# Weight sums of the FFN made with the conversion and kept in DRAM, more conversion in attention, and a new order of FFN group changes

## The chip, the cores and the metric

The kernel runs on one core of a Trainium2 chip. The metric is the device time of one execution in microseconds, lower is better. The kernel before takes 1252.25 us, the median of three runs (1250.42 to 1252.28).

## The reference

Attention with a feature map, a mixture of eight experts of which each chosen token uses one, and an FFN whose hidden layer is the maximum of three products:

```python
# q, k, v: (8, 8, 576, 64); w_phi: (64, 128); x: 4608 tokens of 512; d_ff 1024 (experts), 768 (FFN)
def phi(x):
    proj = np.einsum('bhsd,df->bhsf', x, w_phi)
    proj = proj - np.max(np.abs(proj), axis=-1, keepdims=True)
    return np.concatenate([np.exp(proj), np.exp(-proj)], axis=-1)
q_p, k_p = (phi(q), phi(k))
kv = np.einsum('bhsf,bhsd->bhfd', k_p, v)
num = np.einsum('bhsf,bhfd->bhsd', q_p, kv)
den = np.einsum('bhsf,bhf->bhs', q_p, k_p.sum(2))[..., None] + 1e-06
x = num / den                                   # to 4608 x 512
do_compute = x @ w_skip > 0                     # the other tokens pass unchanged
e_idx, gate_w = argmax and softmax weight of x @ w_gate
x[mask of expert e] += gate_w * (np.maximum(x @ w1[e], 0) @ w2[e])
h = np.maximum(np.maximum(x @ ffn_w1, x @ ffn_w2), x @ ffn_w3)
out = h @ ffn_w_out
```

The FFN's weights come in as float64.

## The kernel before

**Attention** runs in 72 steps and five more to drain. A step makes two tiles of 128 tokens for a pair of heads: projections `pr` on TensorE (L553), their largest absolute value `m` (L558) and the difference `d` (L560) on VectorE, exponentials on ScalarE, then the sums `kv` and the numerators `n` on TensorE, and the division in `put_x` on VectorE. `n` has one PSUM buffer. SP loads the inputs `raw`, three chunks ahead; a chunk serves one and a half steps. After every 18 steps a pair of batches is complete, and `route` (L229 is its first reduction) finds each token's expert; its list positions are scattered by POOL (`scatter_ids`).

**The conversion.** `conv_steps` is a generator that turns the 24 float64 tiles of FFN weights, 128x512 each, into float32 and stores them in `wfd` in DRAM. A tile takes six steps: SP loads `pf`; ScalarE squares the high words into `sq` and VectorE begins `da`; two more VectorE instructions (L190, L195); then VectorE's last (L199), ScalarE's copy of the low words into `sq` (L200) and POOL's multiply and add (L201, L202); an empty step; and the store to `wfd` on SP (L205). `sq` has one buffer, `da` and `pf` two. Sixty steps of attention (6 to 65) call it once each; the rest is called from `pump` in the expert stage. Behind the 24 tiles the same generator makes the overflow lists (`make_overflow`, with one iota on POOL).

**Experts.** The experts are worked off in the order of their sizes, in blocks of up to 384 tokens. For a block POOL gathers the tokens' rows from `xa` in DRAM (`gather`), TensorE transposes them (`xt`), `layer1` makes `ht`, `layer2` the outputs, which VectorE adds to the rows (`add_y`, L964) and POOL scatters back (`put_rows`, L969). Each matmul is made of three (L486 to L488), with operands split into a rounded high and a low part: ScalarE writes the high part, VectorE subtracts it for the low one (`w_split`, L168 and L170). After every second product or so the kernel calls `pump`, which splits one more weight and then makes one step of the conversion. Once all expert weights are split, `pump` makes steps of `w1_prep`, which prepares the FFN's first weights.

**FFN.** It multiplies 2x2 blocks with seven products in place of eight, so that it needs sums of blocks of both operands. `quad1` is one set of seven products for a group of 512 tokens and one pair of weight tiles: nine pairs in each of nine groups, 81 sets; `quad2` does the same for layer 2, 18 sets. For a pair of weight tiles `Operands` loads both tiles from `wfd` into one staging buffer `stg` (of four, shared with the expert weights and `f_load`), has POOL make four sums (`sums_left`, `sums_right`, L804 to L813) into `sc`, and splits one half tile (`single`), one whole (`wide`) and two wholes of sums (`pair`) with `split` (L800 on ScalarE, L801 on VectorE). The products of a set run in the order 6, 4 (of the set before), 1 (of the next one), 5, 7, 2 (of the next one), 3. Products 1, 6, 5 and 3 accumulate in one PSUM buffer and ScalarE copies it to `pu` (L1129) after 1, 6 and 5.

Everything else of the FFN hangs on a list: `do(n, at, f)` has `f` issued behind product `at` of set `n`. `x_next` puts the next group there: `f_load` of its rows, `f_ps` and `f_xt` (two PSUM tiles of `ps_t`, which has two, and eight transposes, L1065) for half `i` = 0 and then for half 1, `x_put` for the splits of the group's operands and `x_sums` for their sums (L1080). The first group is written out by hand ahead of the loop: all transposes, all sums and splits, and then products 1 and 2 of set 0. `w1_prep` goes on with one step behind each product of sets 0 to 4, and with all the rest in set 5. `to_layer2` lists the loads and splits of layer 2's weights and of the first hidden groups in the last group of layer 1.

The order on each engine is the order in which the code issues instructions.

Of the kernel before, what the change touches and what calls it, by code (L numbers as in the profile page):

```python
# [19 lines left out]
P = 128  # L20
# [25 lines left out]
def kernel(  # L46
# [42 lines left out]
    wfd = dram.tile([NFT, P, 512], F32, name="wfd")  # L89

# [89 lines left out]
    def from_double(t, pool, i):  # L180
# [23 lines left out]
        yield  # L204
        nc.sync.dma_start(out=wfd[i], in_=af)  # L205

    conv_done = [0]

    def conv_steps(pool):
# [5 lines left out]
        nxt = start(0)  # L215
# [294 lines left out]
    with ac:  # L510
# [201 lines left out]
        for s2 in range(NS // 2 + LN):  # L712
# [61 lines left out]
    sc_p = ctx.enter_context(tc.tile_pool(name="sc", bufs=2))  # L774
# [28 lines left out]
    def sums_left(sc, x11, x12, x21, x22, eng):  # L803
        eng.tensor_tensor(out=sc[:, 2], in0=x21, in1=x22, op=ALU.add)  # L804
        eng.tensor_tensor(out=sc[:, 0], in0=sc[:, 2], in1=x11, op=ALU.subtract)
        eng.tensor_tensor(out=sc[:, 1], in0=x11, in1=x21, op=ALU.subtract)
        eng.tensor_tensor(out=sc[:, 3], in0=x12, in1=sc[:, 0], op=ALU.subtract)

    def sums_right(sc, x11, x12, x21, x22, eng):
        eng.tensor_tensor(out=sc[:, 2], in0=x12, in1=x11, op=ALU.subtract)  # L810
        eng.tensor_tensor(out=sc[:, 0], in0=x22, in1=sc[:, 2], op=ALU.subtract)
        eng.tensor_tensor(out=sc[:, 1], in0=x22, in1=x12, op=ALU.subtract)
        eng.tensor_tensor(out=sc[:, 3], in0=x21, in1=sc[:, 0], op=ALU.subtract)  # L813

# [12 lines left out]
    class Operands:  # L827


        def __init__(self, raw, side, whole, half, sums, eng=nc.vector):  # L830
            self.raw, self.side, self.whole, self.half, self.pool, self.eng = raw, side, whole, half, sums, eng
            self.blocks = {}

        def steps(self):
            return [self.sums, self.single, self.wide, lambda: self.pair(0), lambda: self.pair(2)]

        def sums(self):
            r = self.raw
            x = [[r[:, a, b * 256 : (b + 1) * 256] for b in range(2)] for a in range(2)]
            self.sc = self.pool.tile([P, 4, 256], F32, name="sc")  # L840
            if self.side == "rows":
                sums_left(self.sc, x[0][0], x[0][1], x[1][0], x[1][1], nc.gpsimd)
            elif self.side == "cols":
                sums_left(self.sc, x[0][0], x[1][0], x[0][1], x[1][1], nc.gpsimd)
            else:
                sums_right(self.sc, x[0][0], x[0][1], x[1][0], x[1][1], nc.gpsimd)

        def single(self):
            h = self.half()
            rows = self.side == "rows"  # L850
            split(h, self.raw[:, 1, 256:] if rows else self.raw[:, 0, 0:256], self.eng)
            self.blocks[4 if rows else 1] = h

        def wide(self):
            w = self.whole()
            split(w, self.raw[:, 0 if self.side == "rows" else 1], self.eng)
            a, b = {"rows": (1, 2), "cols": (2, 4), "right": (2, 3)}[self.side]
            self.blocks[a], self.blocks[b] = w[:, :, 0:256], w[:, :, 256:]

        def pair(self, c):  # L860
            w = self.whole()
            split(w, self.sc[:, c : c + 2].rearrange("p a b -> p (a b)"))
# [384 lines left out]
    def op_step(ops, key, i):  # L1247
        ops[key][i]()
# [217 lines left out]
```

## Time and profile before

| | |
|---|---|
| median of 3 runs | 1252.25 us |
| profiled execution | 1254.91 us, its span 1253.2 us |
| TensorE matmul busy | 1134.4 us, 91% of the span |
| VectorE busy | 853.6 us, 68% |
| ScalarE busy | 562.0 us, 45% |
| POOL (GpSimd) busy | 321.7 us, 26% |
| mean granted TensorE clock | 0.972 of full speed |
| chain that ended last | TensorE 42%, VectorE 6%, DMA 6%, POOL 5%, issue 4%, ScalarE 2% |

PE is TensorE, DVE VectorE, ACT ScalarE, SP the engine that issues most transfers. Attention lasts to about 370 us, the experts to about 655 us, layer 1 of the FFN to about 1090 us. A row's number in brackets is the time for which its engine stood idle ahead of it, with what ended the idle time.

### The profile page before, as it was taken

To read this page: it belongs to the slowest core of one execution; us is meant where nothing else is said; L and a number is where in the kernel's file an instruction comes from. 1 tells how busy PE (TensorE), PEld (TensorE's weight loads), DVE (VectorE), ACT (ScalarE), POOL (GpSimd) and SP (SyncE) were. 2 spreads that over 40 slices of the span, in tenths; PEclk is the share of its full clock that TensorE was granted. 3 is DMA by queue.
4 is the path that set the end of the run, shared out by engine and by line. 5 is a ranking of instruction groups with operands and counts; after the bars stand their busy time and mean duration, and the time that the engine had idled before them with its cause. 6 is when DMAs were issued, how large, how long until landed. Compare 5 with 4: busy or idle time off the path is not lost.

```text
span 1253.2 us, 34023 instructions
## 1 busy us (share of the span) xinstructions
PE 1134.4 (91%) x14212; PEld 1055.3 (84%) x14212; DVE 853.6 (68%) x1820; ACT 562.0 (45%) x1290; POOL 321.7 (26%) x356
## 2 busy tenths in 40 slices
PE   6999899898687889878997899999999999999996
PEld 5888788777576778767886899999999999999996
DVE  5889679778553575776877756556556566887772
ACT  3565555544361344455445333333333233455552
POOL 0001221212164345343154100000000000569770
PEclk9999999999799899989998999999999999999998
DMA  7555845454741665665753120220111111345541
GB/s 260 179 167 184 190 158 189 162 171 129 112 133 31 200 231 159 236 210 176 238 161 92 68 68 35 68 69 35 68 62 41 55 49 50 135 153 188 186 149 70
DMA packets 96782, 166.53 MB, mean 133 GB/s; under 512 B 20674, under 2 KB 39618, under 8 KB 96624
## 3 DMA queue, kind: packets, MB, share of 16 engines
q1 hardware_dynamic: 91904, 154.19, 38.7%
q0 software_dynamic: 4352, 8.85, 2.2%
q8 instruction: 113, 1.85, 0.6%
q10 hardware_dynamic: 368, 1.27, 0.3%
q14 instruction: 45, 0.37, 0.1%
HBM read 120.77 MB, written 45.51 MB: 133 GB/s over the span
## 4 chain that ended last, share of the span: by engine, by line
PE 42%; DVE 6%; DMA 6%; POOL 5%; issue 4%; ACT 2%; POOLq 0%; SPq 0%; ACTq 0%; DVEq 0%
PE mm L488 14%; PE mm L486 14%; PE mm L487 14%; DMA xa<-xg,ixr 4%; DMA stg<-in_w_exp_dram 1%; POOL sq L201 1%; POOL xg L468 1%; DVE sc L1080 1%; PE tp L1065 1%; POOL da L202 1%; DVE wB L801 1%; DVE w L801 1%; DVE xB L801 1%; ACT xB L800 0%; DVE mt L1114 0%
## 5 line engine op out<-in xcount | busy, mean ns | idle before, releaser
L1129 ACT ACTIVATE pu<-mm 128x256 f32<-128x256 f32 x297 | 114.4, 385 | 271.3 <-PE mm L488 248.1
L1116 DVE TENSOR_TENSOR pu<-mm,pu 128x256 f32<-128x256 f32 x162 | 68.2, 421 | 95.0 <-PE mm L488 92.2
L804 POOL TENSOR_TENSOR sc<-stg 128x256 f32<-128x256 f32 x15 | 12.3, 823 | 409.7 <-DMA stg<-hd 375.0
L579 ACT ACTIVATE e<-d 128x512 f32<-128x512 f32 x144 | 82.9, 623 | 62.9 <-DVE d L560 57.4
L633 PE MATMUL n<-kvw,q 128*64 128x74 f32 x2304 | 95.2, 235 | 15.2 <-issue 14.7
L593 PE MATMUL kv<-raw,e 128*64 128x74 f32 (+1 forms) x2560 | 97.6, 234 | 4.1 <-issue 4.0
L593 PEld LDWEIGHTS kv<-raw,e 128*64 128x64 f32 (+1 forms) x2560 | 83.9, 138 | 19.6 <-issue 17.9
L558 DVE TENSOR_REDUCE m<-pr 128x8 f32<-128x1024 f32 x72 | 87.8, 1220 | 18.0 <-PE pr L553 12.6
L633 PEld LDWEIGHTS n<-kvw,q 128*64 128x64 f32 x2304 | 85.0, 141 | 17.7 <-issue 16.4
L553 PE MATMUL pr<-wph,raw 64*64 64x128 f32 x2304 | 87.9, 289 | 9.5 <-DMA wph<-in_w_phi_dram 6.3
L486 PE MATMUL mm<-xT,w 128*128 128x256 f32 x288 | 81.8, 284 | 11.5 <-ACT pu L1129 5.9
L560 DVE TENSOR_TENSOR d<-pr,m 128x1024 f32<-128x1024 f32 x72 | 88.2, 1225 | 4.6
L201 POOL TENSOR_TENSOR sq<-sq,pf 128x512 f32<-128x512 f32 x24 | 31.7, 1319 | 227.8 <-DVE pf L199 205.8
L1114 DVE TENSOR_TENSOR mt<-mm,pu 128x256 f32<-128x256 f32 x135 | 56.4, 417 | 39.3 <-PE mm L488 38.8
L553 PEld LDWEIGHTS pr<-wph,raw 64*64 64x64 f32 x2304 | 68.3, 141 | 16.7 <-DMA raw<-in_qkv_dram 6.3
L572 ACT ACTIVATE q<-tr 128x512 f32<-128x512 f32 x72 | 42.7, 594 | 87.9 <-PE tr L570 81.7
L487 PE MATMUL mm<-xT,w 128*128 128x256 f32 x288 | 81.5, 283 | 0.0
L488 PE MATMUL mm<-xT,w 128*128 128x256 f32 x288 | 81.4, 283 | 0.0
L1117 DVE TENSOR_TENSOR mt<-mt,pu 128x256 f32<-128x256 f32 x162 | 71.8, 443 | 5.6
L487 PE MATMUL mm<-wB,w 128*128 128x256 f32 x266 | 74.5, 280 | 0.0
L488 PE MATMUL mm<-wB,w 128*128 128x256 f32 x266 | 74.5, 280 | 0.0
L486 PE MATMUL mm<-wB,w 128*128 128x256 f32 x266 | 74.4, 280 | 0.0
(278 smaller groups left out, 3800.7 us busy)
## 6 DMA issues: line engine op xcount, KB each, us to landing
raw<-in_qkv_dram SPq DMA_DIRECT2D x46, 798.0 KB
stg<-in_w_exp_dram SPq DMA_DIRECT2D x64, 512.0 KB
hd<-mt SPq DMA_DIRECT2D x27, 512.0 KB
pf<-in_w_ffn_dram SPq DMA_DIRECT2D x24, 512.0 KB
hb<-hd SPq DMA_DIRECT2D x21, 512.0 KB
xa<-xs SPq DMA_DIRECT2D x16, 576.0 KB
stg<-xa SPq DMA_DIRECT2D x18, 512.0 KB
out_dram<-mt SPq DMA_DIRECT2D x18, 512.0 KB
```

The source lines that it names most:

```text
L486: nc.tensor.matmul(out=ps, lhsT=ah, rhs=bh, start=first, stop=False, skip_group_check=on)
L487: nc.tensor.matmul(out=ps, lhsT=ah, rhs=bl, start=False, stop=False, skip_group_check=on)
L488: nc.tensor.matmul(out=ps, lhsT=al, rhs=bh, start=False, stop=last, skip_group_check=on)
L553: nc.tensor.matmul(out=pr[p0 : p0 + 64, h, 2 * s + i], lhsT=raw[k0, o + p0 : o + p0 + 64], rhs=wph[k0], start=True, stop=True,)
L558: nc.vector.tensor_reduce(out=m, in_=pr, axis=AX.X, op=ALU.max, apply_absolute_value=True)
L560: nc.vector.tensor_tensor(out=d, in0=pr, in1=m[:, :, :, None].to_broadcast([P, 2, 4, P]), op=ALU.subtract)
L579: nc.scalar.activation(out=e[:, :, :, s], in_=ds[s2][:, :, 2:4], func=AF.Exp, scale=scale)
L593: nc.tensor.matmul(out=kvps[u, b][c : c + 64, 2 * h + s], lhsT=e[p0:p1, h, i, s, c : c + 64], rhs=v[p0:p1, h], start=t == 4 * b and h + s ...
L633: nc.tensor.matmul(out=ps[p0 : p0 + 64, i, h], lhsT=q[:, s, 2 * h + i, p0 : p0 + 64], rhs=kvw[u, b][:, 2 * h + s], start=s == 0, stop=s == 1,)
L1116: nc.vector.tensor_tensor(out=tmp, in0=ps, in1=tmp, op=ALU.add)
L1117: nc.vector.tensor_tensor(out=out, in0=out, in1=tmp, op=ALU.max)
L1129: nc.scalar.activation(out=t, in_=ps, func=AF.Copy)
```

## The change

- `from_double` loses its empty step: the store to `wfd` follows one step after POOL's instructions. After every second tile POOL makes the pair's four sums into `sm` and SP stores them in a new DRAM tensor `wsm`; that takes two steps, so that a pair still takes twelve.
- Attention makes two conversion steps in each of its 60 steps.
- The FFN's weight operands no longer have POOL make sums. `Operands.load` brings for each pair, in two staging buffers, half of the sums and one tile, and then the other half and half a tile. Hidden operands of layer 2 keep their sums on POOL (`HiddenOperands`).
- `w1_prep` loads one part ahead and is listed behind each product of sets 0 to 7.
- The first group: products 1 and 2 of set 0 come before the second half of the transposes, product 6 of set 0 and product 1 of set 1 among the sums and splits.
- `x_next`: half 1 of a group starts ten products after half 0 where it started seven after.
- `to_layer2`: loads and splits of layer 2's weights in six parts, at other products. The pool `sc` moves from the expert stage to the FFN, and the first group uses it. Pairs of `w_out` tiles lie side by side in the input's layout.

```diff
-    def from_double(t, pool, i):
+    def from_double(t, pool, i, pair):
...
         nc.gpsimd.tensor_tensor(out=sq, in0=sq, in1=hi.bitcast(F32), op=ALU.mult)
         nc.gpsimd.tensor_tensor(out=af, in0=af, in1=sq, op=ALU.add)
         yield
-        yield
         nc.sync.dma_start(out=wfd[i], in_=af)
+        pair.append(af)
...
+    def sums_left(sc, x11, x12, x21, x22, eng):
+        eng.tensor_tensor(out=sc[:, 2], in0=x21, in1=x22, op=ALU.add)
+        eng.tensor_tensor(out=sc[:, 0], in0=sc[:, 2], in1=x11, op=ALU.subtract)
+        eng.tensor_tensor(out=sc[:, 1], in0=x11, in1=x21, op=ALU.subtract)
+        eng.tensor_tensor(out=sc[:, 3], in0=x12, in1=sc[:, 0], op=ALU.subtract)
...
             t, nxt = nxt, start(i + 1) if i + 1 < NFT else None
             yield
-            yield from from_double(t, pool, i)
-            conv_done[0] = i + 1
+            yield from from_double(t, pool, i, pair)
+            if i % 2:
+                yield
+                x = [v[:, c : c + 256] for v in pair for c in (0, 256)]
+                sm = pool.tile([P, 4, 256], F32, name="sm", bufs=1)
+                (sums_left if i < 18 else sums_right)(sm, *x, nc.gpsimd)
+                pair.clear()
+                yield
+                nc.sync.dma_start(out=wsm[i // 2], in_=sm.rearrange("p (a b) c -> p a (b c)", a=2))
+                conv_done[0] = i // 2 + 1
...
             if 6 <= s2 < NS // 2 - 6:
                 next(conv)
+                next(conv)
...
     class Operands:
+        def __init__(self, side, whole, half):
+            self.side, self.whole, self.half, self.blocks = side, whole, half, {}
+
+        def load(self, n, p):
+            right = self.side == "right"
+            t = stg_p.tile([P, 2, 512], F32, name="stg")
+            nc.sync.dma_start(out=t[:, 1 - n] if n == 0 else t[:, 0], in_=wsm[p, :, n])
+            if n == 0:
+                nc.sync.dma_start(out=t[:, 0], in_=wfd[2 * p + right])
+            elif right:
+                nc.sync.dma_start(out=t[:, 1, 0:256], in_=wfd[2 * p, :, 0:256])
+            else:
+                nc.sync.dma_start(out=t[:, 1, 0:256], in_=wfd[2 * p + 1, :, 256:])
+            if n == 0:
+                self.src = [t[:, 0], t[:, 1]]
+            else:
+                self.src += [t[:, 0], t[:, 1, 0:256]]
+
+        def step(self, i):
+            right = self.side == "right"
+            if i == 3:
+                h = self.half()
+                split(h, self.src[3])
+                self.blocks[1 if right else 4] = h
+            else:
+                w = self.whole()
+                split(w, self.src[i])
+                a, b = (((2, 3) if right else (1, 2)), (6, 7), ((5, 4) if right else (5, 3)))[i]
+                self.blocks[a], self.blocks[b] = w[:, :, 0:256], w[:, :, 256:]
...
     def w1_steps():
         half = halves(w1_tile)
+        ops = [Operands("left", w1_tile, half) for _ in range(9)]
+
+        def load(n):
+            p, part = divmod(n, 2)
+            if p < 9:
+                while conv_done[0] <= p:
+                    next(conv)
+                ops[p].load(part, p)
+
+        load(0)
+        yield
         for p in range(9):
-            nxt = load(p + 1) if p < 8 else None
-            yield
...
+            for part in range(2):
+                load(2 * p + part + 1)
+                if part == 0:
+                    while w1_used[0] + 4 > (freed[0] - WF + NWA + NWB if not wc_p else NWA + NWB + NWC + 4):
+                        yield
+                for i in (2 * part, 2 * part + 1):
+                    ops[p].step(i)
+                    yield
+            w1[p] = ops[p].blocks
...
         for i in range(2):
-            q = n0 + 5 + i
-            do(q, 0, f_ps, g, i)
-            do(q, 0, f_xt, g, i)
-            for at, p in ((2, 1), (3, 2), (4, 3)):
-                do(q, at, x_put, g, p, i)
-            do(q, 5, x_sums, g, i, (0,))
-            do(q, 6, x_sums, g, i, (1,))
+            q = 7 * (n0 + 5) + 10 * i
+            at = [divmod(q + t, 7) for t in range(8)]
+            do(*at[0], f_ps, g, i)
+            do(*at[0], f_xt, g, i)
+            for t, p in ((2, 1), (3, 2), (4, 3)):
+                do(*at[t], x_put, g, p, i)
+            do(*at[5], x_sums, g, i, (0,))
+            do(*at[6], x_sums, g, i, (1,))
...
-        for k, (ld, at) in enumerate(((2, 6), (4, 1), (4, 1))):
-            do(n0 + ld, at, w2_load, k)
+        for k, part, q, at in ((0, 0, 2, 6), (0, 1, 3, 1), (1, 0, 4, 0), (1, 1, 5, 0), (2, 0, 5, 5), (2, 1, 5, 5)):
+            do(n0 + q, at, w2_load, k, part)
...
             for p in (1, 2):
                 for i in range(2):
                     x_put(g0, p, i)
+            step(0, 1)
+            step(0, 2)
     for i in range(2):
         x_sums(g0, i, (0,))
     for i in range(2):
         x_put(g0, 6, i)
+    step(0, 6)
     for i in range(2):
         x_sums(g0, i, (1,))
+    step(1, 1)
     for p in (5, 7, 3, 4):
         for i in range(2):
             x_put(g0, p, i)
-    for n in range(5):
+    for n in range(8):
         for at in range(7):
             do(n, at, next, w1_prep, None)
-    do(5, 0, list, w1_prep)
```

## Rows read from the trace of the kernel before

**Rows 1.** Busy time by stretch: matmul, weight load, DVE, ACT, POOL, clock, DMA.

```profile
30.00:345.00 315.00, 284.38 (x7201) 249.36 (x7203) 248.56 (x552) 167.83 (x353) 53.03 (x50) 0.96 0.57 165
...
701.00:1075.00 374.00, 364.44 (x3059) 361.38 (x3058) 223.86 (x572) 128.66 (x362) 4.75 (x6) 1.00 0.17 59
1075.00:1240.00 165.00, 163.75 (x1381) 163.34 (x1380) 126.88 (x212) 90.29 (x210) 106.25 (x115) 1.00 0.43 147
```

**Rows 2.** Timeline of VectorE in attention: start, duration, what (first and last steps).

```profile
61.73 1.23 DVE L558 TENSOR_REDUCE m<-pr 128x8 f32<-128x1024 f32 x1
...
99.34 1.22 DVE L558 TENSOR_REDUCE m<-pr 128x8 f32<-128x1024 f32 x1
...
130.37 1.22 DVE L558 TENSOR_REDUCE m<-pr 128x8 f32<-128x1024 f32 x1
...
133.61 1.22 DVE L558 TENSOR_REDUCE m<-pr 128x8 f32<-128x1024 f32 x1
```

**Rows 3.** TensorE's waits, 470 to 656 us: total, times, longest.

```profile
PE mm L487 <- DVE xt L482: 3.4, 2, 2.0
PE mm L486 <- DVE ht L478: 2.9, 1, 2.9
PE mm L486 <- ACT ht L476: 2.4, 1, 2.4
PE mm L488 <- DVE ht L478: 2.1, 4, 0.8
```

**Rows 4.** TensorE's waits, 701 to 1240 us.

```profile
PE tp L1065 <- DVE sc L1080: 9.6, 16, 1.0
```

**Rows 5.** Timelines of TensorE, ScalarE and POOL where the FFN begins.

```profile
668.69 0.58 PE L486 MATMUL mm<-xT,w 128*128 128x256 f32 x1 [5.92 <-ACT pu L1129]
...
664.42 0.72 ACT L800 ACTIVATE xT<-mt 128x256 fp32r<-128x256 f32 x2 [2.89 <-DMA xa<-xg,ixr]
...
668.25 0.38 ACT L1129 ACTIVATE pu<-mm 128x256 f32<-128x256 f32 x1
...
659.29 1.00 POOL L969 DMA_INDIRECT xa<-xg,ixr  x1
```

**Rows 6.** TensorE's waits, 655 to 701 us.

```profile
PE mm L486 <- DVE pu L1116: 3.0, 1, 3.0
...
PE mm L486 <- DVE mt L1114: 2.0, 1, 2.0
```

**Rows 7.** Groups in attention, 30 to 330 us: busy, mean ns of one, idle before.

```profile
L190 DVE SCALAR_TENSOR_TENSOR da<-pf,da 128x512 int32<-128x512 int32 x10 | 6.8, 681 | 0.0
...
L199 DVE TENSOR_SCALAR pf<-da 128x512 int32<-128x512 int32 x10 | 4.2, 420 | 0.0
...
L229 DVE TENSOR_REDUCE lr<-lg 128x81 f32<-128x648 f32 x3 | 4.1, 1355 | 0.0
...
L184 ACT ACTIVATE sq<-pf 128x512 f32<-128x512 f32 x10 | 6.8, 684 | 0.0
```

**Rows 8.** Splits beside POOL's sums (671 to 701 us), alone (620 to 638); first sum.

```profile
L801 DVE TENSOR_TENSOR wB<-stg,wB 128x256 fp32r<-128x256 f32 x4 | 3.7, 922 | 0.0
...
L801 DVE TENSOR_TENSOR wB<-stg,wB 128x512 fp32r<-128x512 f32 x3 | 3.1, 1032 | 1.1 <-ACT wB L800 1.1
...
L170 DVE TENSOR_TENSOR wB<-stg,wB 128x512 fp32r<-128x512 f32 x11 | 7.0, 686 | 0.1
...
639.00 0.74 POOL L804 TENSOR_TENSOR sc<-stg 128x256 f32<-128x256 f32 x1 [4.65 <-DMA stg<-wfd]
```

**Rows 9.** Timelines of POOL, ScalarE and TensorE at an expert block's end.

```profile
511.81 1.05 POOL L468 DMA_INDIRECT xg<-xa,ixr  x1 [4.16 <-DMA xa<-xg,ixr]
...
515.99 0.66 ACT L184 ACTIVATE sq<-pf 128x512 f32<-128x512 f32 x1 [7.51 <-POOL da L202]
...
516.97 0.50 PE L486 MATMUL mm<-wB,ht 128*128 128x512 f32 x1 [2.40 <-ACT ht L476]
```

**Rows 10.** TensorE's waits, 411 to 470 us.

```profile
PE mm L486 <- ACT ht L476: 4.5, 3, 4.1
```

More of the change, by code (lines that the diff above doesn't have):

```diff
@@ L89 @@
     wfd = dram.tile([NFT, P, 512], F32, name="wfd")
+    wsm = dram.tile([NFT // 2, P, 2, 512], F32, name="wsm")
     def setup(load):
@@ L213, in start @@
             return t
-        nxt = start(0)
+        nxt, pair = start(0), []
         for i in range(NFT):
@@ L827 @@
     class Operands:
[L830 to L837, printed above, removed]
+        def __init__(self, side, whole, half):
+            self.side, self.whole, self.half, self.blocks = side, whole, half, {}
@@ new lines, in step, with __init__ @@
+        def step(self, i):
[9 more added lines that the diff above has]
+                self.blocks[a], self.blocks[b] = w[:, :, 0:256], w[:, :, 256:]
+    class HiddenOperands:
+        def __init__(self, raw, whole, half, pool):
+            self.raw, self.whole, self.half, self.pool, self.blocks = raw, whole, half, pool, {}
+        def step(self, i):
@@ L848, in single @@
[L848 to L858, printed above, removed]
@@ L876, in w1_steps @@
         half = halves(w1_tile)
-        def load(p):
-            while conv_done[0] < 2 * p + 2:
-                next(conv)
-            t = stg_p.tile([P, 2, 512], F32, name="stg")
-            nc.sync.dma_start(out=t, in_=wfd[2 * p : 2 * p + 2].rearrange("i p c -> p i c"))
-            return Operands(t, "rows", w1_tile, half, sc_p)
-        cur, nxt = load(0), None
+        ops = [Operands("left", w1_tile, half) for _ in range(9)]
[6 more added lines that the diff above has]
+        load(0)
         yield
-        cur.sums()
         for p in range(9):
-            nxt = load(p + 1) if p < 8 else None
-            yield
-            while w1_used[0] + 4 > (freed[0] - WF + NWA + NWB if not wc_p else NWA + NWB + NWC + 4):
-                yield
-            for f in cur.steps()[1:]:
-                f()
-                yield
-                if f == cur.wide and nxt:
-                    nxt.sums()
-            w1[p] = cur.blocks
-            cur = nxt
+            for part in range(2):
[7 more added lines that the diff above has]
+            w1[p] = ops[p].blocks
     w1_prep = w1_steps()
@@ L1196 @@
     w2_op = {}
-    def w2_load(k):
-        raw = stg_p.tile([P, 2, 512], F32, name="stg")
-        nc.sync.dma_start(out=raw, in_=wfd[18 + k : 24 : 3].rearrange("i p c -> p i c"))
-        op = Operands(raw, "right", lambda: wb_p.tile([P, 2, 512], F32R, name="wB"), w2_half, sc_p)
-        w2[k], w2_op[k] = op.blocks, op.steps()
+    for k in range(3):
+        w2_op[k] = Operands("right", lambda: wb_p.tile([P, 2, 512], F32R, name="wB"), w2_half)
+        w2[k] = w2_op[k].blocks
     h_used = [0]
@@ L1245, in x_next, with w2_load @@
             do(n0 + 9, 2 + i, x_put, g, 4, i)
+    def w2_load(k, part):
+        w2_op[k].load(part, 9 + k)
     def op_step(ops, key, i):
-        ops[key][i]()
+        ops[key].step(i)
     def to_layer2(n0):
@@ L1269, in to_layer2 @@
                 do(n0 + q, at, op_step, w2_op, k, i)
[L1270 to L1271 removed]
+        for k, (q, at) in enumerate(((6, 5), (6, 5), (7, 5))):
+            do(n0 + q, at, h_load, g1, k, stg, "stg", sb_p)
     def layer2_pools():
@@ L1290, in h_next, with step @@
                     do(*at[first + k], op_step, h_op, (g, k), s)
+    quads = [(quad1, g, p) for g in groups for p in range(9)] + [(quad2, g, m) for g in groups for m in range(2)]
+    made = {}
+    def step(n, p):
+        if 0 <= n < len(quads):
+            if n not in made:
+                f, *args = quads[n]
+                made[n] = f(*args)
+            made[n].step(p)
     g0 = groups[0]
```

72 lines of the change are left out of this document (25 added, 47 removed), and 6 rows, old and new, of tables (at, q).

## The prediction

> **What bounds the kernel now.** I read the page's first two parts, then busy time by stretch, then TensorE's waits in each stretch, and last the order of instructions at the places where TensorE stood. Three stretches differ. In attention TensorE is busy for 284.4 of 315 us, VectorE for 248.6 [rows 1]; where nothing disturbs them, nine steps take 37.61 us, 4.18 us each, and VectorE needs 3.24 us for a step that carries no conversion [rows 2]. So TensorE sets the pace there, and VectorE has a little under a microsecond to spare. In the expert stage TensorE waits for evictions: its releasers are `ht` and `xt`, which ScalarE and VectorE write [rows 3]. In the FFN it is busy for 364.4 of 374 us [rows 1], and 9.6 of the missing microseconds are one wait, 16 times [rows 4]. Layer 2 is full (163.75 of 165 us) [rows 1]. The time to be won lies in the second stretch, at the turn from experts to FFN [rows 5, 6], and in that one repeated wait.
>
> **Attention: ten more tiles converted there.** Sixty steps convert ten tiles now and twenty after. A tile has two VectorE instructions of 0.68 us and two of 0.42 us, 2.20 us, and two on ScalarE of 0.68 us, 1.37 us [rows 7]. That is 22 us more VectorE and 13.7 us more ScalarE work in 60 steps, 0.37 us of VectorE a step. A step has 3.24 us without conversion, some 0.1 us more where a new chunk is read, and would then have 0.73 us of conversion: 4.1 us on average against TensorE's 4.18 [rows 2]. It just fits, so most of it is hidden under TensorE. It fits badly in steps with both 0.68 us instructions, and beside routing, whose first reduction alone has 1.36 us, once for each of three pairs [rows 7]: what VectorE is late there TensorE's single `n` buffer passes on. I take one such reduction's length for each of the three, 4 us. Below that the bound is 0 (all hidden; nothing leaves this stretch that could make it shorter); above, everything exposed, 22 + 13.7 = 36 us; the row it is nearest to is the 3.24 us step with its 0.9 us of room, so I stay near the low end and let 12 us stand as the end of what is likely. The POOL sums (4 of 0.74 us or more for each pair) [rows 8] run while POOL is nearly idle (53 of 315 us) [rows 1]. The `wfd` store moves to one conversion step after POOL's add where it stood two behind, and holds SP's later `raw` loads while it waits; those are issued three chunks, four and a half steps or 18.8 us, ahead, which hides POOL's two instructions. If that cover went, the next late thing would be `ones_col` on ScalarE, then TensorE.
>
> The Trainium skill (SBUF — State Buffer, "Who interferes with whom") says that a VectorE instruction with two SBUF inputs and a GpSimd instruction that reads SBUF exclude each other, the later one blocked until the other ends. The trace agrees in part: the same subtraction takes 1.03 us beside POOL's sums and 0.69 us alone [rows 8], so a meeting costs 0.35 us and not a whole POOL instruction. By the rule, putting sums beside attention would move the sum by the price given under the second rival below.
>
> **Experts: ten tiles less converted there.** One such place shows the pattern [rows 9]. At a block's end POOL waits for the scatter to land, then gathers, and only then runs the conversion's multiply and add, which stood behind in its queue; ScalarE's next `Square` needs that buffer and waits 7.51 us; the eviction of `ht` is queued behind it on ScalarE, and TensorE stands 2.40 us. With the change four tiles of fourteen are left to convert here, and the overflow's dozen steps: 36 steps of 96. One is made with each pump, so the four tiles are through after a quarter of the time that conversion now takes, before the stretch that starts at 470 us. The waits for evictions in that stretch are 3.4 + 2.9 + 2.4 + 2.1 = 10.8 us [rows 3]: conversion instructions stand in front of each `xt` and `ht`, and the 2.9 us is VectorE waiting for the overflow's iota, queued on POOL behind gathers. I count all of it. Of the 4.5 us before 470 us [rows 10] I count half, 2.2 us, since the conversion step that meets the block's end becomes another one. Against it stand two pairs' sums, 3 to 4 us each on POOL, in front of gathers, and SP's weight loads behind the `wsm` store; I take 1 us. Term: -12 us. Bounds: -15 (all of both) and -3 (only the iota's wait goes, and POOL's queue makes the others anew). SP's queue also loses ten `pf` loads and ten `wfd` stores in front of weight loads, which I leave at nothing: TensorE waits for no weight there.
>
> **The turn to the FFN.** Product 6 starts at 668.69 us because it continues the sum that product 1 left, whose eviction ScalarE makes at 668.25 us, behind ten splits of `xT` and `xB` [rows 5]. The new order evicts product 1 right after it. Then `xT` decides: ScalarE begins it at 664.42 us, so with VectorE's half it is there by 665.7 us: 3 us earlier. Moreover `xT` itself waited for the last scatter [rows 5], which POOL issued at 659.29 us behind sums of its own, while the `add_y` that it waits for stood on VectorE behind splits slowed by the same sums; both go, 2 us more. Against it, `f_load`'s second tile takes a staging buffer that a weight part holds longer, and queues on SP behind two more loads; I take 1 us. Term: -4; bounds -6 and -1.
>
> **Weight operands of layer 1.** Here TensorE waits 3.0 + 2.0 us for VectorE [rows 6], which makes splits slowly there: three wholes and four halves from staging into `wB` cost 3.1 + 3.7 us, where wholes at 0.69 us and halves at half of that and a little more, 0.42 us, would cost 3.7 us in all [rows 8]. Without POOL's sums beside them VectorE gets 3.1 us back from these seven alone, and three splits more (2 us) are done before the FFN begins, together the 5 us that it was late. What is new is loading: 896 KB in four transfers for each pair instead of 512 KB in one, through the same four staging buffers, and the first of them is issued only when a split has freed one. The nearest row is POOL's wait of 4.65 us for the first such load [rows 8]; 2.1 us of it are hidden by the three products between two evictions of one sum (a product is six matmuls, 0.71 us by 364.4 us for 3059 of them) [rows 1], 2.5 us not. Term: -5 + 2.5 = -2.5; bounds -5 (all hidden) and +2 (three such loads late).
>
> **Group changes.** The second half's transposes wait for the first half's sums, 16 times, 9.6 us [rows 4]. The change puts three more products between them. At 0.71 us a product that is 2.1 us against a longest wait of 1.0 us. I count 9; bounds -9.6 and -6 (VectorE late in one group of three). The later sums and splits keep their places before first use.
>
> **Layer 2.** Three `w2` sums leave POOL, six loads replace three, splits move by a few products. TensorE is full [rows 1] and each load is issued at least nine products before its first split, 6.4 us: 0, at worst +2.
>
> **Sum.** +4 - 12 - 4 - 2.5 - 9 + 0 = -23.5 us. The profiled execution took 1254.91 us, 1253.2 of span and 1.7 around it, 2.66 us above the median of 1252.25; 1254.91 - 23.5 = 1231.4, which for the median is 1229.
>
> **Rivals.** First, *the experts' waits form anew*: fewer conversions, but POOL's chain of scatter, wait and gather stays, and each wait removed lets TensorE reach the next one. For it: each block's end has that chain [rows 9]. Against: evictions, not gathers, are the releasers [rows 3]. With -3 there and attention at +8: 8 - 3 - 4 - 2.5 - 9 = -10.5, 1242 us. Second, *sums on POOL hold up attention*: one meeting for each of 20 tiles, at the 0.74 us of a POOL sum [rows 8], 15 us, all exposed: -23.5 + 15 = -8.5, 1244 us. For it: the slowed splits. Against: the cost there is half. This is what the rule cited above would make. Third, *the FFN's start gains nothing*: loads come late (+2) and the prologue gains 1: 4 - 12 - 1 + 2 - 9 = -16, 1236 us. Fourth, the other side: *VectorE and ScalarE become attention's pace*. All 36 us are exposed: 36 - 12 - 4 - 2.5 - 9 = +8.5, 1261 us. It decides once attention loses more than the 27.5 us won elsewhere, 0.46 us for each of 60 steps, which means a step of 4.64 us instead of 4.18. For it: VectorE would be busy for 98 of 100. Against: the 0.9 us of room. That the group change doesn't remove its wait would cost 9 of the 23.5 us, inside the range.
>
> **How the numbers follow.** Forecast 0.60, first rival 0.16, second 0.06, third 0.12, fourth 0.06. The predicted time is 1229 us. The lower bounds of all terms give 0 - 15 - 6 - 5 - 9.6 = -36, 1216 us; the upper end, 1245 us, takes in the first three rivals. Range 1216 to 1245 us. A difference under 0.2%, 2.5 us, can't be told from none here. Faster by more: 0.90 (all but the fourth rival and the worst of the others); within it 0.03; slower 0.07.
>
> **What would show it.** Right: the 16 waits of the transposes are gone; VectorE's idle time in attention is smaller but the L558 starts stay near 4.2 us apart; no `Square` waits for POOL after some 470 us; product 6 of the first group follows its `xT` at once and no longer an eviction. Wrong: L558 starts over 4.6 us apart in undisturbed attention; TensorE waiting for `pu` evictions while ScalarE waits for a load from `wsm`; new waits for gathers among the experts.

## The result, and the profile after

The changed kernel takes 1219.55 us (median of 4 runs, 1216.43 to 1220.35) where the kernel before takes 1251.61 (4 runs): a ratio of 0.972, 95% interval 0.968 to 0.976. The prediction was 1229 us, range 1216 to 1245. The profiled execution takes 1219.28 us, 1217.6 of it span, 35.6 less span than the profiled one of before; that is the difference to be placed, against the -23.5 us of the sum (the medians differ by 32.1, as the profiled execution of before lay 3.3 above the median given here and that of the changed kernel 0.3 below its own).

Line numbers below are those of the changed kernel (`m` L580, `xt` and `ht` L498 to L504, conversion L185 to L205, pair sums L210 to L219, FFN transposes L1091). The first view is busy time by stretch, cut at the same places of the program: from `m` of step 6 to the last `m`; from the third routing count to the FFN's first transpose; to the 28th `pu` eviction; to the 244th, where layer 2 is under way. First the changed kernel:

```profile
29.24:354.43 325.19, 287.28 (x7288) 252.62 (x7288) 277.11 (x598) 177.42 (x375) 112.18 (x115) 0.96 0.67 201
381.30:639.64 258.34, 237.24 (x1431) 210.20 (x1431) 157.20 (x304) 110.05 (x230) 79.63 (x99) 0.96 0.57 181
639.64:698.61 58.97, 54.72 (x400) 52.71 (x401) 42.65 (x104) 29.12 (x78) 0.00 (x0) 0.90 0.35 115
698.61:1071.23 372.62, 372.11 (x3141) 371.78 (x3140) 236.69 (x593) 139.38 (x383) 9.91 (x12) 1.00 0.21 71
```

The same of the kernel before:

```profile
30.05:348.80 318.75, 288.13 (x7299) 252.69 (x7300) 250.78 (x559) 169.43 (x355) 56.25 (x54) 0.96 0.56 163
375.38:657.38 282.00, 243.01 (x1431) 209.25 (x1431) 183.71 (x341) 121.63 (x247) 115.31 (x124) 0.96 0.57 182
657.38:722.48 65.10, 52.53 (x400) 51.09 (x401) 50.84 (x108) 30.65 (x81) 19.59 (x24) 0.92 0.25 80
722.48:1106.82 384.34, 374.73 (x3142) 371.64 (x3141) 239.94 (x592) 139.04 (x382) 21.05 (x24) 1.00 0.19 65
```

The reader is to see four things. Up to the third count the changed kernel is 5.9 us late (381.30 for 375.38). The experts then take 23.7 us less, of which 17.9 are TensorE's idle time (39.0 to 21.1) and 5.8 its busy time for the same 1431 matmuls. The FFN's start takes 6.1 less, layer 1 another 11.7 less. Layer 2 is as long as before (135.0 and 135.1 us). Together -35.5.

What was listed as the signs: the starts of `m` that answer to the first two of [rows 2], nine steps apart, are 4.40 us a step here and not 4.18, between the sign for right (near 4.2) and the one for wrong (over 4.6) (timeline of VectorE):

```profile
62.97 1.22 DVE L580 TENSOR_REDUCE m<-pr 128x8 f32<-128x1024 f32 x1
...
102.57 1.22 DVE L580 TENSOR_REDUCE m<-pr 128x8 f32<-128x1024 f32 x1
```

TensorE's waits in attention (30 to 345 us) have new releasers, where before only one of 2.6 us had a name:

```profile
PE n L633 <- DVE lg L678: 4.7, 3, 2.5
PE n L655 <- DVE sm L306: 3.2, 3, 1.1
...
PE tr L592 <- ACT q L595: 2.3, 3, 1.0
PE n L633 <- DVE xs L674: 2.2, 1, 2.2
```

`lg`, `xs` and `sm` are VectorE's: its division and its routing come late, as the first term said. These four rows are 12.4 us; for most of TensorE's idle time in attention the profile names no releaser. The waits of the expert stage (381 to 640 us), which answer to [rows 3, 10]:

```profile
PE tp L515 <- DMA xg<-xa,ixr: 9.0, 1, 9.0
PE mm L509 <- DVE xt L504: 5.1, 2, 2.6
PE tp L1091 <- DMA stg<-xa: 4.3, 1, 4.3
PE mm L510 <- DVE ht L500: 1.2, 2, 0.7
...
PE mm L508 <- ACT ht L498: 0.9, 2, 0.7
```

and the same stretch of the kernel before (375 to 658 us), of which [rows 3, 10] were parts:

```profile
PE tp L493 <- DMA xg<-xa,ixr: 16.8, 3, 10.2
PE mm L486 <- ACT ht L476: 6.9, 4, 4.1
PE mm L487 <- DVE xt L482: 4.4, 3, 2.0
PE mm L488 <- DVE ht L478: 3.0, 6, 0.8
PE mm L486 <- DVE ht L478: 2.9, 1, 2.9
```

ScalarE's last `Square` starts at 456.49 us, so that none waits for POOL after 470, and TensorE's waits for gathers are one where they were three. The 16 waits of [rows 4] are gone; between 701 and 1075 us one wait is left, of 0.5 us, for `mt`. At the turn product 6 follows its `xT`, as against [rows 5], but the transposes wait 4.34 us for their rows where they waited 2.51 (timeline of TensorE):

```profile
639.64 1.09 PE L1091 MATMUL tp<-ident,stg 128*128 128x128 f32 x4 [4.34 <-DMA stg<-xa]
...
646.55 0.38 PE L508 MATMUL mm<-xT,w 128*128 128x256 f32 x1 [1.02 <-ACT xT L822]
```

### The profile page after: what moved, and what is told of

Its sections match the earlier page's. It is cut to its first block, busy times and chain, and to the rows that moved or that the text cites. A ratio compares the mean times of both kernels' runs of the same rounds, so it can differ in the third digit from the quotient of the medians.

```text
span 1217.6 us, 34130 instructions
## 1 busy us (share of the span) xinstructions
PE 1126.7 (93%) x14212; PEld 1057.5 (87%) x14212; DVE 841.8 (69%) x1820; ACT 557.0 (46%) x1290; POOL 310.5 (25%) x356
## 4 chain that ended last, share of the span: by engine, by line
PE 56%; DMA 3%; DVE 2%; POOL 1%; issue 1%; ACT 1%; SPq 0%; POOLq 0%; DVEq 0%; ACTq 0%
PE mm L509 18%; PE mm L510 18%; PE mm L508 18%; PE tp L1091 1%; DMA xa<-xg,ixr 1%; DMA stg<-xa 1%; DVE w L823 1%; PE tp L515 0%; POOL xg L490 0%; DMA stg<-wfd 0%; POOL da L203 0%; DMA stg<-in_w_exp_dram 0%; POOL sq L202 0%; DVE wC L823 0%; DVE pu L1138 0%
## 5 line engine op out<-in xcount | busy, mean ns | idle before, releaser
L210 POOL TENSOR_TENSOR sc<-stg 128x256 f32<-128x256 f32 x6 | 5.1, 844 | 428.0 <-DMA stg<-hd 398.0
L615 PEld LDWEIGHTS kv<-raw,e 128*64 128x64 f32 (+1 forms) x2560 | 82.8, 137 | 18.1 <-issue 16.8
L580 DVE TENSOR_REDUCE m<-pr 128x8 f32<-128x1024 f32 x72 | 87.7, 1218 | 13.1 <-PE pr L575 10.4
L508 PE MATMUL mm<-xT,w 128*128 128x256 f32 x324 | 92.5, 285 | 3.2 <-ACT xT L822 1.8
L575 PE MATMUL pr<-wph,raw 64*64 64x128 f32 x2304 | 84.7, 286 | 8.8 <-DMA wph<-in_w_phi_dram 7.3
L509 PE MATMUL mm<-xT,w 128*128 128x256 f32 x324 | 91.8, 283 | 0.3 <-DVE xT L823 0.3
L510 PE MATMUL mm<-xT,w 128*128 128x256 f32 x324 | 91.3, 282 | 0.0
L508 PEld LDWEIGHTS mm<-xT,w 128*128 128x128 f32 x324 | 61.7, 191 | 4.5 <-ACT xT L822 2.3
```

What stands on the lines that cost most here:

```text
L508: nc.tensor.matmul(out=ps, lhsT=ah, rhs=bh, start=first, stop=False, skip_group_check=on)
L509: nc.tensor.matmul(out=ps, lhsT=ah, rhs=bl, start=False, stop=False, skip_group_check=on)
L510: nc.tensor.matmul(out=ps, lhsT=al, rhs=bh, start=False, stop=last, skip_group_check=on)
L575: nc.tensor.matmul(out=pr[p0 : p0 + 64, h, 2 * s + i], lhsT=raw[k0, o + p0 : o + p0 + 64], rhs=wph[k0], start=True, stop=True,)
L580: nc.vector.tensor_reduce(out=m, in_=pr, axis=AX.X, op=ALU.max, apply_absolute_value=True)
L615: nc.tensor.matmul(out=kvps[u, b][c : c + 64, 2 * h + s], lhsT=e[p0:p1, h, i, s, c : c + 64], rhs=v[p0:p1, h], start=t == 4 * b and h + s ...
```

## The experiments

Ratios are to the kernel before in the same session, with 95% intervals. The stage lengths are those of the profiled executions, cut as above; idle is the length less TensorE's matmul time.

| kernel | ratio | attention, idle | experts, idle | FFN start | layer 1 |
|---|---|---|---|---|---|
| before | 1 | 318.8, 30.6 | 282.0, 39.0 | 65.1 | 384.3 |
| changed | 0.972 (0.968 to 0.976) | 325.2, 37.9 | 258.3, 21.1 | 59.0 | 372.6 |
| changed, again | 0.975 (0.971 to 0.980) | 329.0, 38.1 | 256.4, 19.3 | 58.3 | 372.3 |
| e1 group order alone | 0.991 (0.988 to 0.995) | 324.3, 29.1 | 281.9, 35.5 | 64.5 | 373.7 |
| e2 two conversion steps alone | 0.976 (0.973 to 0.979) | 327.7, 36.1 | 249.4, 15.9 | 64.3 | 384.3 |
| e6 both, no stored sums | 0.969 (0.966 to 0.972) | 326.5, 33.6 | 248.7, 15.4 | 63.1 | 373.2 |
| e9 e6, product 1 early | 0.972 (0.967 to 0.976) | 314.5, 33.0 | 250.3, 16.4 | 60.0 | 373.2 |
| e10 e6, calls apart | 0.977 (0.973 to 0.982) | 327.4, 43.9 | 250.2, 16.6 | 62.6 | 373.6 |
| e3 changed, one step | 1.002 (0.999 to 1.005) | 316.1, 28.9 | 310.0, 56.9 | 58.1 | 372.6 |
| e4 changed, FFN start as before | 0.976 (0.973 to 0.979) | 330.0, 40.2 | 258.7, 22.1 | 57.3 | 372.7 |
| e5 changed, stores later | 0.971 (0.966 to 0.975) | 327.4, 38.6 | 254.4, 20.8 | 58.6 | 372.6 |
| e7 changed, all 24 tiles | 0.974 (0.970 to 0.977) | 329.9, 43.6 | 247.1, 12.5 | 58.1 | 372.6 |
| e11 the same in fewer steps | 0.979 (0.975 to 0.983) | 337.8, 51.6 | 246.0, 14.2 | 57.7 | 372.6 |
| e12 changed, GpSimd's queue | 0.975 (0.970 to 0.979) | 334.2, 40.8 | 259.6, 21.3 | 59.1 | 372.5 |

e1 to e4, the changed kernel's second run with e5 to e7, and e9 to e11 each shared a chip.

**e1, the group order alone**, in the kernel before:

```
-            q = n0 + 5 + i
-            do(q, 0, f_ps, g, i)
+            q = 7 * (n0 + 5) + 10 * i
+            at = [divmod(q + t, 7) for t in range(8)]
+            do(*at[0], f_ps, g, i)
...
```

> The kernel before with one part of the change: the second half of each group change begins ten products behind the first half, not seven. Theory (the prediction's term): the 16 waits of the transposes for VectorE's sc go (9.6 us) and nothing takes their place, -9 us, 1251.6 - 9 = about 1242.6 us, and no wait of over 0.3 us at the transposes. Rival: VectorE is late by its whole queue there, the wait shows again at the transposes or at a product that needs xB or xT, under 3 us are won, 1249 us or more.

Measured: 0.991, 11 us; layer 1 takes 373.7 us for 384.3. Idle time there falls from 9.6 to 1.5 us, and the busy time for 3142 matmuls from 374.7 to 372.2. The theory holds, and the term was a little small.

**e2, two conversion steps alone**, in the kernel before:

```
             if 6 <= s2 < NS // 2 - 6:
                 next(conv)
+                next(conv)
```

> The kernel before with one part of the change: two conversion steps for each attention step, so 20 tiles are converted there and 4 in the expert stage; the weight sums stay on GpSimd in the FFN's preparation. Theory: the conversions themselves are what made TensorE wait among the experts; attention +4 to +6 us, experts about -20, together -14 to -16, 1235 to 1238 us, with TensorE's waits between 470 and 600 us gone and no Square that waits for GpSimd there. Rival (the prediction's size): the experts give -12, together -6 to -8, 1244 to 1246 us. Second rival: what went among the experts went because GpSimd no longer makes the FFN's sums there; then this kernel gains nothing there and takes 1255 us or more.

Measured: 0.976, 30 us by the medians, more than any theory said (the two profiled executions differ by 23.2 us: attention takes 8.9 us more in e2's). The second rival falls. This one line is the largest part of the change: the experts fall by 32.6 us to this row:

```profile
386.07:635.48 249.41, 233.53 (x1431) 207.01 (x1431) 162.16 (x301) 108.39 (x227) 86.50 (x104) 0.98 0.55 173
```

Idle time falls by 23.1 us. The waits of that stretch tell where from: for `ht` from 12.8 to 2.3 us, for `xt` from 5.5 to 0.9, for gathers from 16.8 to 10.1. Busy time for the same 1431 matmuls falls by 9.5, at a granted clock of 0.98 for 0.96.

**e3, one step in the changed kernel** (the second `next(conv)` taken out):

> The changed kernel with one part undone: one conversion step for each attention step, so ten tiles (five pairs with their sums) are converted in attention and seven pairs with their sums in the expert stage. Theory (conversions cost among the experts): attention -5 us, experts +20 or more, since seven pairs' sums on GpSimd stand before gathers there, together +15 to +22, 1235 to 1242 us, and the Square waits for GpSimd's da are back to some 30 us. Rival (the gain among the experts came from the sums kept in DRAM): attention -5, experts 0 to +3, 1214 to 1218 us.

Measured: 1.002, as slow as before. The rival falls. The theory has the sign and misses the size: attention idles 9 us less, but the experts take 51.7 us more than with two steps, where 20 or more were expected, and ScalarE's `Square` waits there 45.0 us for POOL's `da` (9.4 in the changed kernel). With ten tiles more (32.6 us by e2) go five more pairs' sums; how the other 19 us divide between these and the FFN's weights, which cannot be prepared before their sums are stored, was not taken apart.

**e4, the FFN's start as before**, in the changed kernel:

```
-            step(0, 1)
-            step(0, 2)
...
-    step(0, 6)
...
-    step(1, 1)
     for p in (5, 7, 3, 4):
...
+    step(0, 1)
+    step(0, 2)
     for n in range(len(quads)):
```

> The changed kernel with one part undone: products 1 and 2 of set 0, product 6 and the next set's product 1 are issued behind the whole preparation of the first group, as before, not in between. Theory (the prediction's): product 6 waits again for the eviction of product 1, which stands behind ten splits on ScalarE, 3 to 5 us, 1222.5 to 1224.5 us. Rival: the first group's xT is what comes last anyway, and the order changes under 1 us, 1219 to 1220.5 us.

Measured: 0.976, beside 0.972 and 0.975 for the changed kernel. The mechanism is there, the time is not: product 6 starts 3.2 us late, right after product 1's eviction (which ends at 654.81; the view names no releaser),

```profile
654.91 0.55 PE L508 MATMUL mm<-xT,w 128*128 128x256 f32 x1 [3.23 <-issue]
```

but the whole start takes 57.3 us, not more than the 58.3 and 59.0 of the changed kernel. There product 6 and the one behind it wait for `xT`, 1.02 + 0.31 + 0.78 us, and over the whole start TensorE idles as long: 4.5 us in e4, 4.3 and 4.7 in the changed kernel. By the stage the rival holds; the ratio alone can't tell the two apart.

**The changed kernel again**, for the chip of the next three:

> The changed kernel again, to stand on the same chip as the three that follow. Its ratio to the kernel before was 0.972 with an interval of 0.968 to 0.976; both theories expect the same here.

Measured: 0.975; stage by stage it is within 2 us of its first profile, except for attention (329.0 for 325.2 us, with the same idle time).

**e5, the conversion's stores two steps later**, in the changed kernel, and `wsm`'s likewise:

```
-        nc.sync.dma_start(out=wfd[i], in_=af)
+        due.append([3, lambda: nc.sync.dma_start(out=wfd[i], in_=af)])
```

> The changed kernel; each conversion store (to wfd and to wsm) is issued two conversion steps later, with the same number of steps. Theory: what is left of waits among the experts comes from SP's queue: the wfd store waits there for GpSimd's da, which stands behind a gather, and the expert weight loads stand behind the store (the 17 us of SP, the 10.3 us of ScalarE for stg and TensorE's two waits of 2.5 and 2.6 us for xt). Then both of those waits go with the clock they cost, 5 to 7 us faster than the changed kernel, experts (from the third routing count to the FFN's first transpose) 251 to 253 us in place of 258. Rival: the pairs' sums on GpSimd in front of the gathers cost it; then under 1.5 us are won and the xt waits stay.

The question is what the two 2.5 us waits for `xt` come from. In the changed kernel the timelines of POOL, VectorE, TensorE, SP and ScalarE show two chains:

```profile
447.44 0.74 POOL L219 TENSOR_TENSOR sm<-da,sm 128x256 f32<-128x256 f32 x1
...
447.51 0.95 DVE L187 TENSOR_SCALAR da<-pf 128x512 int32<-128x512 int32 x1 [2.15 <-POOL sm L218]
...
452.78 0.39 PE L509 MATMUL mm<-xt,wB 128*128 128x256 f32 x1 [2.53 <-DVE xt L504]
...
465.65 1.05 POOL L490 DMA_INDIRECT xg<-xa,ixr  x1 [3.45 <-DMA xa<-xg,ixr]
...
470.82 1.28 POOL L203 TENSOR_TENSOR da<-da,sq 128x512 f32<-128x512 f32 x1
...
472.13 0.33 SPq L205 DMA_DIRECT2D wfd<-da  x1
472.71 0.38 SPq L152 DMA_DIRECT2D stg<-in_w_exp_dram  x1
...
476.64 0.63 ACT L169 ACTIVATE wB<-stg 128x512 fp32r<-128x512 f32 x1 [10.26 <-DMA stg<-in_w_exp_dram]
...
481.26 0.58 PE L509 MATMUL mm<-xt,wB 128*128 128x256 f32 x1 [2.58 <-DVE xt L504]
```

First chain: VectorE's next `da` needs a buffer that the pair's sums still read; the wait stands in VectorE's queue ahead of `xt`. Second chain: POOL waits for a scatter before its gather, the conversion's add stands behind, SP waits 12.3 us for that add with the `wfd` store, the expert weight load stands behind the store, ScalarE waits 10.26 us for the weight, and `xt` stands behind the split. That the wait is SP's is what the Trainium skill says too (DMA: Bandwidth & Descriptors, "Anatomy of one DMA — SWDGE (gpsimd) path"): a DMA engine waits for no semaphore, the sequencer that issues does, before it sends the transfer off. The 12.3 us are the trace's number for it, and that the wait holds what SP issues next is seen in the trace: the weight load goes out at 472.71, right behind the store.

In e5 two weight loads go ahead of the late store, and the second wait for `xt` is gone; the first stays (timelines of TensorE and SP):

```profile
456.89 0.39 PE L522 MATMUL mm<-xt,wB 128*128 128x256 f32 x1 [2.54 <-DVE xt L517]
...
464.39 2.00 SPq L152 DMA_DIRECT2D stg<-in_w_exp_dram  x2
477.94 0.34 SPq L205 DMA_DIRECT2D wfd<-da  x1
```

So each theory was right for one of the two waits. But the experts take 254.4 us, 2 won of the 5 to 7 expected: elsewhere SP now stands 15.7 us for a `pf` load whose buffer POOL still reads, and waits for `ht` (1.4 us more) and gathers (1.6) stand where the `xt` wait was; idle time is 20.8 us (19.3 and 21.1 in the changed kernel's two profiles), and what is won is busy time, 233.6 for 237.1 us. The ratio, 0.971, can't be told from the changed kernel's 0.975.

**e6, the change without its stored sums and its FFN start**: e1 and e2 together.

> The kernel before with two conversion steps for each attention step and the new group order, but the weight sums still made by GpSimd in the FFN's preparation and the FFN's start as before: the change without its stored sums. Theory (the parts add up): experts 249 us as with two steps alone, the turn and the first weights 6 us longer than in the changed kernel, group changes as there, together 2 to 4 us faster than the changed kernel. Rival: the stored sums earn their place at the start of the FFN; then this kernel is 4 to 8 us slower than the changed one.

Measured: 0.969 beside 0.975 on the same chip (1216.47 and 1225.57 us); the intervals overlap a little. The stages add up as the theory said: experts 248.7, FFN start 63.1, layer 1 373.2. What the stored sums win at the start of the FFN (4 to 5 us) they lose among the experts (8 to 10 us) and in attention.

**e7, all 24 tiles in attention steps 2 to 73**, in the changed kernel:

```
-            if 6 <= s2 < NS // 2 - 6:
+            if 2 <= s2 < NS // 2 + 2:
```

> The changed kernel with the conversion called twice in attention steps 2 to 73 in place of 6 to 65: 144 steps, so all 24 tiles with all sums are made before the experts, where only the overflow lists remain. Theory (conversions and their stores are what is left of waits among the experts): attention +3 us for four tiles more, experts -8, together 4 to 6 us faster than the changed kernel. Rival: the last steps of attention, with the routing of the third pair, have no room left; attention +8 or more, and nothing is won.

Measured: 0.974. The experts fall to 247.1 us as expected, and attention takes it back: step 6 begins 2 us later, idle time grows by 5.5 (this trace has some 50 matmul records fewer, which is part of it), and from the last `m` to the third count it is 31.8 us in place of 27. The rival holds.

**e9, e6 with product 1 of set 0 early** (`step(0, 1)` behind the first half of the transposes):

> The kernel without stored sums (two conversion steps, new group order, GpSimd's weight sums as before: ratio 0.9691 to the kernel before), with product 1 of set 0 and its eviction issued behind the first half of the transposes. Theory: there product 6 waits 5.1 us for that eviction; the wait falls to 1 or 2 us, as xT is next, and 3 us are won, ratio 0.966 to 0.967, some 1213 us. Rival, as where the order was undone in the changed kernel: the time moves to the next waits (pu by VectorE 3.4 us, the clock), ratio 0.968 to 0.970.

Measured: in the stage the theory, 60.0 us for 63.1, the wait for `pu` 1.8 us in place of 5.1; in the time nothing that can be told (0.972, e6 0.969).

**e10, e6 with the two calls apart** (one `next(conv)` moved to behind `st_proj`):

> The kernel without stored sums, with the two conversion calls of an attention step set apart: one behind the projections, one at the end. Theory: attention's loss of some 8 us for the second call comes from two long VectorE instructions one behind the other ahead of m; apart they cost 3 to 4 us less, attention 322 to 324 us from step 6 to step 71 in place of 326 to 330, ratio 0.966. Rival: what counts is the sum of VectorE's and ScalarE's work, or the one ahead of the division holds n; then 0 to +4 us, ratio 0.969 to 0.972.

Measured: 0.977; attention idles 43.9 us where e6 idles 33.6. The rival holds: the same step costs more ahead of the division than behind it.

**e11, all 24 tiles in steps 6 to 65** of the changed kernel:

```
-                next(conv)
-                next(conv)
+                for _ in range(3 if s2 % 5 in (0, 2) else 2):
+                    next(conv)
```

> The changed kernel with all 24 tiles and their sums converted in attention steps 6 to 65, three calls in two of five steps and two in the others, so the last steps of attention carry none. Theory: attention +3 us, experts -9 as where they were converted over all steps (247 in place of 256 to 258), and the 5 us that routing lost there are not lost here: 5 to 6 us faster than the changed kernel, ratio 0.970 to 0.971. Rival: a third call in a step is more than VectorE has room for, 24 times some 0.4 us; attention +10, no gain, ratio 0.975 or more.

Measured: 0.979. Experts 246.0 us, attention's idle time 51.6 in place of 38: 13.5 us for 24 third calls, 0.56 each. The rival holds in time. That VectorE has no room is not shown: it waits there itself, seven times and 14.0 us in total, for a buffer `da` that the pair's sums on POOL still read. First e11, then the changed kernel (VectorE's waits, 30 to 345 us):

```profile
DVE da L187 <- POOL sm L213: 14.0, 7, 2.7
```

```profile
DVE da L187 <- POOL sm L213: 0.4, 1, 0.4
```

More `da` buffers, which would part the two, were not tried.

**e12, the conversion's transfers on GpSimd's queue** (`nc.gpsimd.dma_start` for `pf`, `wfd` and `wsm`), in the changed kernel:

> The changed kernel with the conversion's three kinds of transfer (pf loads, wfd and wsm stores) issued on GpSimd's queue in place of SP's, so nothing on SP waits for GpSimd's arithmetic. With later stores the wait had moved from the store to the pf load behind it on SP, 15.7 us, which waits for the same GpSimd instructions. Theory (SP's queue is what is left of waits among the experts): the expert weight loads no longer stand behind it, both xt waits of 2.5 us are gone, experts 249 to 252 us in place of 256 to 258, ratio 0.967 to 0.970. Rival: GpSimd's own issues stand in front of its gathers and of its multiplies and cost there what SP wins; experts 255 us or more, ratio 0.974 or more.

Measured: 0.975, experts 259.6 us: the rival's time. ScalarE's 10 us for the expert weight are gone, and with them the second wait for `xt`; in its place TensorE waits for the gather (timeline of TensorE):

```profile
465.85 0.39 PE L509 MATMUL mm<-xt,wB 128*128 128x256 f32 x1 [3.01 <-DVE xt L504]
...
486.94 1.09 PE L515 MATMUL tp<-ident,xg 128*128 128x128 f32 x4 [2.35 <-DMA xg<-xa,ixr]
```

The first wait stays, as it comes from the sums.

## Why the prediction was right, and where it was not

**Attention, +4 (0 to +12).** The third count comes 5.9 us later. Since attention's length differs by more than that between executions of the same code (last section), its idle time is the better measure: 29 to 31 us with one call (before, e1, e3), 33 to 36 with two (e2, e6, e9), 38 to 40 with two and the pairs' sums (changed, twice, e4, e5). So the conversions cost about 4 us, the size that was said, and the stored sums, taken at nothing, about 4 more, with up to 3 us between runs of the same attention code. That routing is what makes the 4 us is not shown: TensorE's waits behind its `sm` are 3.2 us in the changed kernel and 0.7 in e2. Why the sums cost their 4 us is open: with one call they cost nothing (28.9 in e3, five pairs with sums), and later stores don't help (38.6 in e5). VectorE isn't slowed by them: its two-input conversion instruction takes 687 ns where it took 681 [rows 7], in this row of the changed kernel's groups (30 to 345 us: busy, mean ns, idle before):

```profile
L191 DVE SCALAR_TENSOR_TENSOR da<-pf,da 128x512 int32<-128x512 int32 x20 | 13.7, 687 | 0.3
```

The second rival, 15 us, is out. The Trainium skill's rule on that port (SBUF — State Buffer, "Who interferes with whom") lengthens such instructions where they meet; the mean of this row, 687 for 681 ns, shows next to nothing of it. The fourth rival is out for two calls; a third has its cost (e11), whether from the pace of VectorE and ScalarE or from the buffer.

**Experts, -12 (-15 to -3): the step that failed.** It measured -23.7, outside its own bounds, and is two errors of opposite sign. The ten tiles less are worth -32.6 (e2), not -13. I had counted the waits for `xt` and `ht` from 470 us on and half of those before; these came out at 15.1 us. I left out the later gather waits (6.7 us by e2), though the first rival spoke of that chain. The reading "evictions, not gathers, are the releasers" was wrong: in the very view of [rows 3] (before, 470 to 656 us) the longest row is a gather's,

```profile
PE tp L493 <- DMA xg<-xa,ixr: 6.6, 2, 6.4
```

and it goes with the conversions. I also had no term for TensorE's busy time, 9.5 us of the same matmuls. Against that, the stored sums cost 8.9 us (changed against e2), where I took 1: waits for `xt` 4.2, the later `f_load` 2.0, busy time 3.7, with 1.1 back from the gather. Half of the `xt` part is the store on SP's queue, which I had looked at for attention and, for the experts, only for its `wsm` part. So a quarter of the gain was lost again, but hardly as the first rival had it: the chain of scatter, gather and conversion stands behind one new wait, the second for `xt` (2.6 us), and no new wait for a gather came.

**The turn, -4, and the weight operands, -2.5.** Together -6.1, at the two places named. But the reason was half wrong: the new order gives nothing that can be measured (e4); the stage is shorter because POOL's sums are gone: with the old order in both, it takes 57.3 us without them (e4) and 63.1 with them (e6), and VectorE's splits of wholes into `wB`, 1032 ns in [rows 8], take 687 (changed kernel, 639.64 to 698.61 us):

```profile
L823 DVE TENSOR_TENSOR wB<-stg,wB 128x512 fp32r<-128x512 f32 x7 | 4.5, 687 | 1.0 <-ACT wB L822 1.0
```

Where those sums stay, the early product is worth 3 us of the stage (e9). `f_load`'s delay, taken at 1 us, is 1.8 (4.34 for 2.51) and counts among the experts here. The third rival is out.

**Group changes, -9 (-9.6 to -6).** Right in mechanism, -11.7 in the changed kernel and -10.6 in e1. The bound was too tight: in e1, beside 8.1 us of idle time, 2.5 us of busy time went.

**Layer 2, 0.** Right.

**Sum.** +5.9 - 23.7 - 6.1 - 11.7 + 0.1 = -35.5, where +4 - 12 - 6.5 - 9 + 0 was said. Nearly the whole miss is the experts' term. That the time stayed inside the range is in part luck: the experts went 8.7 us and the group changes 2.1 us below their own lower bounds, and the range held them only because its low end took every lower bound at once, 0 for attention and -11 for the turn and the operands, where +5.9 and -6.1 came out.

Of the change's three parts, then, the two small edits carry the gain: e1 times e2 is 0.968, e6 measured 0.969, the whole change 0.972 to 0.975. The stored sums, most of the diff, win nothing on balance. Whether e6 is faster than the changed kernel is likely and not shown.

## What to carry to other kernels

Background work is priced by the queues it stands in, not by its busy time: look at what is issued behind each of its instructions and stores on every engine, and move it to the stage where nothing that decides stands behind. When such a move is costed, count the waits of the whole stage that have that work in their chain, gathers and loads too, and give TensorE's busy time a term of its own, since the same matmuls get shorter when the waits go. The next step of such work need not cost what the last one did: the third call cost 0.56 us where the second cost under 0.1 (4 us for 60), and the trace showed it waiting for a buffer, which no count of busy time tells.

## What the runs showed of the hardware

TensorE's busy time for the same work depends on the granted clock. For the experts' 1431 matmuls it is 253.2 us at a mean clock of 0.91 (e3), 246.4 at 0.94 (e1), 243.0 and 237.2 at 0.96 (before, changed), and 233.5 at 0.98 (e2). The records have two levels of the clock, full and half (2.4 and 1.2 GHz). So a mean of 0.91 over e3's 310.0 us means that 27.9 us of full speed were lost; with that taken off its busy time, and the same done for the others, 225 to 232 us remain in all five (an estimate from these rows). The clock was low where TensorE waited: here are four stretches of 10 us of the changed kernel, the first and the last with a wait for `xt` of 2.5 us in them, the two between without. The second is fully busy and still has some of the low level:

```profile
446.00:456.00 10.00, 7.47 (x38) 6.41 (x37) 6.30 (x11) 3.53 (x8) 5.31 (x6) 0.89 0.74 239
456.00:466.00 10.00, 10.00 (x79) 9.96 (x79) 9.97 (x21) 7.72 (x19) 2.90 (x4) 0.94 0.65 221
466.00:476.00 10.00, 10.00 (x49) 8.18 (x48) 2.62 (x9) 0.38 (x2) 8.57 (x12) 1.00 0.39 123
476.00:486.00 10.00, 7.12 (x37) 6.21 (x36) 8.35 (x24) 2.16 (x5) 1.24 (x2) 0.83 0.74 236
```

So waits that go can take busy time with them: in e2 it was 9.5 us beside 23.1 us of idle time.

The mean clock differs between executions of the same code. On one chip, six runs of the changed kernel took 1211.74 to 1227.16 us, at a clock of 0.983 in the fastest and 0.973 in the slowest. In attention, here are e6 and e9, whose attention is the same (two chips):

```profile
30.52:357.01 326.49, 292.88 (x7289) 256.64 (x7289) 274.62 (x598) 178.95 (x375) 81.41 (x73) 0.95 0.61 183
```

```profile
29.77:344.25 314.48, 281.45 (x7286) 247.64 (x7286) 273.86 (x598) 178.53 (x375) 80.53 (x72) 0.98 0.64 189
```

Idle time is the same (33.6 and 33.0 us; 36.1 in e2, with the same attention), busy time differs by 11.4 us. The length of this stage in one profile can't tell a few microseconds; TensorE's idle time tells them better, to some 3 us.
